# Loading the operands of a two-part sequence kernel through the crossbar transpose, with wide VectorE operations and a reordered prologue

## Chip, cores, metric

One core of one Trainium2 chip. The metric is device time of one execution in microseconds (us), lower is better; a figure for a kernel is the median of its executions. The kernel before takes 432.6 us (431.3 to 433.7). The profile is of one execution. The engines are PE (TensorE matmul), DVE (VectorE), ACT (ScalarE), POOL (GpSimd) and SP (SyncE, which here does nothing but issue loads).

## The reference, cut to what matters

Two independent parts are computed in one launch, all in bf16, S = 2048 positions, D = 1024 channels.

```python
# part A: 4-tap convolution of k, product with v, long convolution by FFT, product with q
for t in range(4): k_shift += k_pad[:, t:t+S, :] * shift_k[:, 3-t]
kv  = k_shift * v
y   = irfft(rfft(kv, 2S) * rfft(ssm_k, 2S))[:S] + kv * ssm_D
a   = q * y
# part B: diagonal complex state-space layer with 1024 states
Lam_bar = exp(dt * Lam);  B_bar = ((Lam_bar - 1) / Lam)[:, None] * Bmat
h_t = Lam_bar * h_{t-1} + B_bar x_t          # scan over the 2048 positions
y_t = 2 Re(C h_t) + x_t * Dskip
out = concat(a, y)
```

## The kernel before

Part B works on 16 chunks of 128 positions. For each chunk PE multiplies x by B ("u matmuls", tile `pu`), DVE rotates u by a table, runs a scan and rotates back (giving `h`), and PE multiplies `h` by C ("y matmuls", tile `py`). Part A runs in three stages: 16 rows of taps on DVE (`acc`) with first transforms (A1), a middle stage with 32 groups (A2: matmuls, a product on DVE with two halves swapped by a DMA, matmuls), and a last stage (A3). Both parts are laid into "ticks" (steps of the program's own schedule), and each engine executes its instructions in program order. B, C and x must reach PE with the contracted axis on partitions, so they have to be transposed.

```python
def b_load_x(i):                                   # x, before: plain load, PE transpose, ACT copy
    xn = xpool.tile([P, D], BF16, name="xn", bufs=3)
    dma(xn[:], x[i * T:(i + 1) * T, :])            # dma = a load issued by SP
    # ...
def b_xT(i, eng="s"):
    # ...
    for dd in range(ND):
        nc.tensor.transpose(pt[:, dd, :], xn[:, dd * P:(dd + 1) * P], ident[:])
    nc.scalar.copy(xT[:], pt[:])                   # or nc.vector.tensor_copy
# B (16 blocks) and C (16 blocks) likewise: bt_prep, ct_load / ct_prep

# rotation of one chunk: 12 operations of 1024 elements, two scans, small ones
nc.vector.tensor_mul(st["ta"][:], u[:, 0, :, :], ci[:])
nc.vector.tensor_mul(st["tb"][:], st["u"][:, 1, :, :], si[:])
nc.vector.tensor_add(st["ta"][:], st["ta"][:], st["tb"][:])
# ... three more, then
nc.vector.tensor_tensor_scan(fl(st["ta"]), fl(rtab), fl(st["ta"]), 0.0, ALU.mult, ALU.add)
# ... the scan of tb, the carry, and six more of 1024 for the rotation back

# taps of one row: 4 multiplies and 3 adds of 1024, then the product with v

# prologue: x(0) and B one block at a time, u of chunk 0 behind them; the parameters
# and tables between; then the tap rows and the filter rows (hk)
b_xT(0, "v")
for j in range(NJ):
    bt_prep(j, 0, "v"); bt_prep(j, 1, "s")
    if j >= 1: b_u(0, j - 1, 0); b_u(0, j - 1, 1)
    if j == 1: params_rest()
# ...
gen_tables_b()
```

## Time and profile before

| | before |
|---|---|
| time | 432.6 us (431.3 to 433.7) |
| PE busy | 380.7 us (88%) |
| DVE busy | 350.7 us (81%) |
| ACT busy | 303.6 us (70%) |
| first rotation of part B begins | 37.3 us |
| A2 (second stage of part A) begins | 190.4 us |

No engine is full all along, so the total shares say little; the span has to be cut into stages. First, of the page of the kernel before: the busy lines, and the rows that cut the span into 40 slices of 10.8 us, each digit the busy share in tenths.

```profile
PE 380.7 (88%) x3713; PEld 259.7 (60%) x3713; DVE 350.7 (81%) x642; ACT 303.6 (70%) x531; POOL 130.2 (30%) x224
...
PE   2589799797987997999899999999899999997784
...
DVE  2989999999999999936897979797959637976830
...
GB/s 247 285 255 309 336 289 254 265 240 249 276 235 205 167 163 159 120 334 238 229 241 263 217 247 245 265 234 295 195 217 181 165 69 135 298 176 396 403 316 73
```

DVE reads 8 or 9 from the second slice to the seventeenth (11 to 183 us), PE mostly 9 afterwards. The same in four windows chosen by milestones (prologue; the stage of taps and rotations; the end of A1; A2 to the last matmul). After the window and its length come busy us of PE, PEld, DVE, ACT and POOL with counts, then the granted clock, the DMA share and GB/s.

```profile
0.00:40.00 40.00, 24.48 (x320) 22.32 (x321) 29.26 (x97) 25.86 (x43) 5.32 (x13) 0.91 0.83 267
40.00:180.00 140.00, 123.09 (x1437) 96.35 (x1435) 138.56 (x238) 117.16 (x197) 66.58 (x102) 0.98 0.71 235
180.00:190.40 10.40, 10.40 (x133) 8.04 (x131) 3.98 (x10) 3.26 (x5) 0.00 (x0) 1.00 0.69 225
190.40:425.40 235.00, 222.41 (x1833) 132.98 (x1831) 178.92 (x299) 156.72 (x286) 57.80 (x108) 0.99 0.72 239
```

From 40 to 180 us DVE works 138.6 of 140 us: that stage is DVE-bound. From 190 us on PE works 222 of 235. What the change wants to remove is in these groups (count, busy us, mean ns of one): the transposes of B, C and x on PE, the copy of x on ACT, and narrow DVE operations.

```profile
L409 DVE TENSOR_TENSOR m<-krow,wbc 128x1024 bf16<-128x1024 bf16 x48 | 32.4, 675 | 0.0
...
L263 ACT COPY xT<-pt 128x1024 bf16<-128x1024 bf16 x15 | 15.9, 1060 | 1.7 <-PE pt L259 1.7
...
L601 PE MATMUL pt<-ident,bn 128*128 128x128 bf16 x128 | 12.4, 258 | 6.4 <-ACT BT L605 3.6 <-DMA bn<-in_B_B_im_dram 1.9 <-DVE BT L603 0.6
...
L618 PE MATMUL pt<-ident,bn 128*128 128x128 bf16 x128 | 10.6, 219 | 2.3 <-DMA bn<-in_B_C_im_dram 1.1 <-DMA bn<-in_B_C_re_dram 1.1
L259 PE MATMUL pt<-ident,xn 128*128 128x128 bf16 x128 | 10.3, 225 | 1.1 <-DMA xn<-in_B_x_dram 1.1
```

The loads are issued by SP's queue. Its timeline (start, length of the issue) shows that a plain 256 KB load holds that queue for 0.3 to 0.6 us:

```profile
3.14 0.36 SPq L85 DMA_DIRECT2D xn<-in_B_x_dram  x1
3.54 0.43 SPq L85 DMA_DIRECT2D bn<-in_B_B_re_dram  x1
4.02 0.59 SPq L85 DMA_DIRECT2D bn<-in_B_B_im_dram  x1
```

### The profile page before, as it was taken

To read this page: it belongs to the slowest core of one execution; us is meant where nothing else is said; L and a number is where in the kernel's file an instruction comes from. 1 tells how busy PE (TensorE), PEld (TensorE's weight loads), DVE (VectorE), ACT (ScalarE), POOL (GpSimd) and SP (SyncE) were. 2 spreads that over 40 slices of the span, in tenths; PEclk is the share of its full clock that TensorE was granted. 3 is DMA by queue.
4 is the path that set the end of the run, shared out by engine and by line. 5 is a ranking of instruction groups with operands and counts; after the bars stand their busy time and mean duration, and the time that the engine had idled before them with its cause. 6 is when DMAs were issued, how large, how long until landed. Compare 5 with 4: busy or idle time off the path is not lost.

```text
span 431.1 us, 9757 instructions
## 1 busy us (share of the span) xinstructions
PE 380.7 (88%) x3713; PEld 259.7 (60%) x3713; DVE 350.7 (81%) x642; ACT 303.6 (70%) x531; POOL 130.2 (30%) x224
## 2 busy tenths in 40 slices
PE   2589799797987997999899999999899999997784
PEld 2578687575765875775556566566465666763331
DVE  2989999999999999936897979797959637976830
ACT  1977999787886887646678877878568783344451
POOL 4000344464654455311222232322122211012121
PEclk9979999999999899999999999999899999999989
DMA  7879987778776544397778687879666523959981
GB/s 247 285 255 309 336 289 254 265 240 249 276 235 205 167 163 159 120 334 238 229 241 263 217 247 245 265 234 295 195 217 181 165 69 135 298 176 396 403 316 73
DMA packets 41353, 102.23 MB, mean 237 GB/s; under 512 B 6621, under 2 KB 8925, under 8 KB 41306
## 3 DMA queue, kind: packets, MB, share of 16 engines
q1 hardware_dynamic: 27322, 58.60, 42.7%
q0 software_dynamic: 13984, 43.01, 28.8%
q8 instruction: 29, 0.48, 0.5%
q14 instruction: 18, 0.15, 0.1%
HBM read 59.64 MB, written 33.55 MB: 216 GB/s over the span
## 4 chain that ended last, share of the span: by engine, by line
PE 42%; DVE 28%; issue 12%; DMA 10%; ACT 5%; POOL 2%; SPq 0%; POOLq 0%; DVEq 0%; ACTq 0%
PE pu L274 13%; PE py L345 13%; DVE m L409 5%; PE psa L508 5%; DVE acc L410 4%; DMA hb<-ha 3%; PE psa L533 3%; PE psa L532 3%; DVE ta L305 2%; DVE tb L308 2%; DVE acc L414 2%; DMA out_dram<-ot 2%; POOL out_dram L88 2%; DMA bn<-in_B_C_re_dram 1%; PE pt L601 1%
## 5 line engine op out<-in xcount | busy, mean ns | idle before, releaser
L274 PE MATMUL pu<-xT,BT 128*128 128x128 bf16 x2048 | 156.1, 222 | 0.5 <-ACT xT L263 0.3
L274 PEld LDWEIGHTS <-BT 128*128 128x128 bf16 x2048 | 136.2, 100 | 33.5 <-issue 2.4
L345 PE MATMUL py<-CT,h 128*128 128x512 bf16 x512 | 140.2, 382 | 2.3 <-ACT yo L355 2.3
L345 PEld LDWEIGHTS <-h 128*128 128x128 bf16 x512 | 46.7, 98 | 45.5 <-issue 4.9
L88 POOL DMA_DIRECT2D hb<-ha x64 | 33.4, 526 | 88.9 <-ACT ha L509 85.0
L534 ACT CAST vsb<-psa 128x512 bf16<-128x512 f32 x64 | 37.0, 602 | 25.7 <-PE psa L533 24.8
L88 POOL DMA_DIRECT2D Ys_h<-ysbh x64 | 45.6, 716 | 30.8 <-ACT ysbh L475 29.4
L277 ACT CAST u<-pu 128x512 bf16<-128x512 f32 x64 | 39.4, 615 | 13.2 <-PE pu L274 13.1
L428 ACT CAST ysb<-psa 128x512 bf16<-128x512 f32 x64 | 38.5, 644 | 13.7 <-PE psa L427 13.3
L519 DVE TENSOR_TENSOR ha<-x,ha 128x1024 bf16<-128x1024 bf16 x32 | 21.9, 684 | 27.8 <-DMA hb<-ha 18.7
L475 ACT CAST ysbh<-psa 128x512 bf16<-128x512 f32 x64 | 38.7, 641 | 5.5 <-issue 2.3
L509 ACT CAST ha<-psa 128x512 bf16<-128x512 f32 x64 | 36.8, 598 | 7.3 <-PE psa L508 6.3
L509 ACT CAST x<-psa 128x512 bf16<-128x512 f32 x64 | 36.9, 593 | 7.3 <-PE psa L508 5.2
L308 DVE TENSOR_TENSOR_SCAN tb<-rtab,tb 128x1024 bf16<-128x1024 f32 x16 | 36.6, 2285 | 0.0
L305 DVE TENSOR_TENSOR_SCAN ta<-rtab,ta 128x1024 bf16<-128x1024 f32 x16 | 36.5, 2280 | 0.0
L427 PE MATMUL psa<-acc,F1t 128*128 128x512 bf16 x64 | 24.6, 392 | 12.0 <-DVE acc L414 11.9
L564 ACT CAST ot<-psa 128x512 bf16<-128x512 f32 x32 | 17.9, 589 | 24.4 <-DMA out_dram<-ot 14.8
L409 DVE TENSOR_TENSOR m<-krow,wbc 128x1024 bf16<-128x1024 bf16 x48 | 32.4, 675 | 0.0
L410 DVE TENSOR_TENSOR acc<-acc,m 128x1024 bf16<-128x1024 bf16 x48 | 32.3, 673 | 0.0
L532 PE MATMUL psa<-ha,wts 128*128 128x512 bf16 x64 | 24.5, 384 | 4.2 <-DVE ha L519 4.0
L88 POOL DMA_DIRECT2D Ys_kv<-ysb x32 | 17.8, 557 | 33.9 <-ACT ysb L428 33.9
L350 PE MATMUL py<-Dd,xT 128*128 128x128 bf16 x128 | 28.0, 219 | 0.0
(139 smaller groups left out, 628.5 us busy)
## 6 DMA issues: line engine op xcount, KB each, us to landing
Ys_kv<-ysb POOLq DMA_DIRECT2D x32, 256.0 KB, 2.9
Ys_h<-ysbh POOLq DMA_DIRECT2D x64, 128.0 KB, 3.3
l2k<-Ys_kv SPq DMA_DIRECT2D x16, 512.0 KB, 6.0
l2h<-Ys_h SPq DMA_DIRECT2D x16, 512.0 KB, 4.2
hb<-ha POOLq DMA_DIRECT2D x64, 128.0 KB, 3.7
Vs<-vsb POOLq DMA_DIRECT2D x16, 512.0 KB, 5.9
vv<-Vs SPq DMA_DIRECT2D x32, 256.0 KB, 6.6
xn<-in_B_x_dram SPq DMA_DIRECT2D x16, 256.0 KB, 4.3
```

The costliest lines, as they stand in the source:

```text
L88: return nc.gpsimd.dma_start(out_, in_)
L274: nc.tensor.matmul(pu[:, c, jl, :], BT[:, j, c, dd, :], xT[:, dd, :], start=(dd == 0), stop=(dd == ND - 1))
L277: nc.scalar.copy(u[:, :, j - 1:j + 1, :], pu[:])
L305: ops.append(lambda: nc.vector.tensor_tensor_scan(fl(st["ta"]), fl(rtab), fl(st["ta"]), 0.0, ALU.mult, ALU.add))
L308: nc.vector.tensor_tensor_scan(fl(st["tb"]), fl(rtab), fl(st["tb"]), 0.0, ALU.mult, ALU.add)
L345: nc.tensor.matmul(py[:], h[:, c, j, :], CT[:, j, c, dh * 512:(dh + 1) * 512], start=(j == 0 and c == 0), stop=(j == NJ - 1 and c == 1))
L409: ops.append(lambda jj=jj: nc.vector.tensor_mul(st["m"][:], krows[n2 - jj][:], wbc[:, jj, :]))
L410: ops.append(lambda: nc.vector.tensor_add(st["acc"][:], st["acc"][:], st["m"][:]))
L428: nc.scalar.copy(ysb[:, dh * 512:(dh + 1) * 512], pt[:])
L475: nc.scalar.copy(ysbh[:, :, n2l, :], pt[:].rearrange("p (c d) -> p c d", c=2))
L509: nc.scalar.copy(d_[:, dh * 512:(dh + 1) * 512], pt[:])
L532: nc.tensor.matmul(pt[:], wts[:, gi, 1, :], ha[:, dh * 512:(dh + 1) * 512], start=True, stop=False)
```

## The change

The intent: take 384 of 512 transposes off PE and their copies off ACT by loading x, B and C through the DMA's crossbar transpose (a load that transposes its data on the way in); do the rotations and taps in fewer, wider DVE operations; and fill the prologue with three chunks of u and three tap rows instead of one chunk. The step lengths of A1, A2 and A3 in ticks are set anew. The diff, cut to its core:

```diff
+    def b_load_x(i):
+        xT = xpool.tile([P, ND, T], BF16, name="xT", bufs=XT_BUFS)
+        nc.sync.dma_start_transpose(xT[:], x[i * T:(i + 1) * T, :])
+    def bt_load(j, c):
+        nc.sync.dma_start_transpose(BT[:, j, c, :, :], Bv[c][:, j, :])
+    def ct_load(c, hf):                                   # four loads of 1 MB
+        nc.sync.dma_start_transpose(CT[:, :, c, hf * 512:(hf + 1) * 512], Cv[c][hf * 512:(hf + 1) * 512, :])
-    def b_xT(i, eng="s"): ...   def bt_prep(j, c, eng): ...   def ct_prep(c, dd, eng): ...
@@ rotation: one multiply of 4096 by a table window, one add of 2048, instead of six of 1024
+            s_ = src[:].rearrange("p b j t -> p (b j t)").unsqueeze(1).to_broadcast([P, 2, 2 * W])
+            nc.vector.tensor_mul(m, s_, win(Z))
+            nc.vector.tensor_add(g, m[:, :, 0, :], m[:, :, 1, :])
@@ taps: four rows of k in a ring, one multiply of 4096, an add of 2048, an add of 1024
+            nc.vector.tensor_mul(st["m"][:, 0:h0, :], kring[:, s0:s0 + h0, :], wbc[:, 0:h0, :])
@@ A2 product: x16 by both halves in one multiply of 2048
+        nc.vector.tensor_mul(hab[:], x16[:].unsqueeze(1).to_broadcast([P, 2, D]), hab[:])
@@ steps (ticks): taps 2 -> 3, filter 2 -> 2.5, A2 2 -> 1.5, A3 1 -> 2; chunks of u in the prologue 1 -> 3
@@ prologue: loads of x(0..2) and all of B first; three tap rows on POOL's queue; then
+    params_pre(); gen_tables_a(); run(kvo(0)); params_rest()
+    pro_u(0); pro_mm(0); params_tabs(); run(kvo(1)); gen_tables_b()
+    pro_u(1); pro_mm(1); run(kvo(2)); pro_u(2); pro_mm(2); pro_u(3)
+    a1h_load(0)                                           # filter rows, behind 19 crossbar loads
+    for n2 in (3, 4): a1_load_k(n2, dma); a1_load_v(n2, dma)
+    for hf in range(2):
+        for c in range(2): ct_load(c, hf)
```

## The prediction

> **What bounds it now.** No single engine. The page gives PE 88%, DVE 81%, ACT 70% of 431 us. The table of stretches splits this: from 40 to 180 us DVE is at 19.2-20.0 of every 20 us while PE has 16-19.6 (the stage of conv taps plus state-space rotations: DVE-bound); from 180 to 360 us PE is at 17.6-20.0 and DVE at 7.6-18 (PE-bound, DMA share about 0.8 at 250 GB/s); before 40 us (PE 24.5 of 40, chain of waits through loads of B, PE transposes, ACT copies of BT and wbc) and after 380 us (PE 38 of 51, DMA 0.7-0.8) nothing is full. PE's true occupancy, from back-to-back cadences in the chain (16 pu matmuls 0.89 us, 4 py matmuls 0.86 us, 8 transposes 0.62 us), is an estimate of 369 us, so PE is the floor.
>
> **What the change does.**
> - PE: 384 of 512 transposes (x, B, C) go, about 27 us by cadence; 8 wbc broadcast matmuls come, +2. Estimate 369 -> 343 us.
> - ACT: xT, CT, BT, wbc copies go (15.9+18.0+8.1+4.1 us), 8 small wbc copies come: 304 -> about 263.
> - DVE: a 1024-wide bf16 multiply starts every 0.60 us in the timeline, of which, by the 128-wide ones (0.16-0.25 us), about 0.07 is fixed: 4096 wide = estimate 2.2 us, 2048 = 1.13. Rotation of one chunk: 12x0.60 + two scans (4.6) + 8 tiny ops, about 12.7 -> 2.2+1.13+4.5+2.2+1.13+0.25 = 11.5. Taps of one row 4.8 -> 4.5. Product 1.2 -> 1.13. All DVE: about 348 -> 322.
> - DMA: same bytes (12 MB now through the transpose path). The Trainium skill, "DMA: Bandwidth & Descriptors", section "Latency and other measured facts", gives 261 GB/s for DMA transposes with a non-contiguous middle dimension, about 350-400 contiguous; no trace of this case shows it yet. With the 250-310 GB/s that plain loads reach here, I estimate at most +10 us of DMA time, spread out.
> - Order: three u chunks and three kv rows in the prologue; products step 1.5 ticks instead of 2, the final output stage step 2 instead of 1, so it overlaps the state-space part to the end.
>
> **On the critical path.** Prologue: about 39 us as before until the first rotation, but with two more u chunks and about two more kv rows done (10-14 us gained). DVE-bound stage: 13x4.5 + 5.5x11.5 = 121 us instead of 140 or so; second stage starts near 175 us instead of 190. After it PE has an estimated 183-190 us and DMA 57 MB at 285-300 GB/s (190-200 us): both nearly full, about 205 us with losses. Total about 386 us.
>
> **Predicted** 386 us, 80% range 370 to 410. Faster by over 2%: 0.92; within 2%: 0.05; slower: 0.03.
>
> **What would show it.** Group list: no transposes but those of hk; 4096-wide multiplies at 2.2-2.3 us; scans unchanged. Stretches: PE over 15 of 20 us from 10 us on, DVE full to about 165 us, PE full afterwards, PE over 17 of 20 in the last 50 us. DMA issues: transposed 256 KB loads landing in 4-7 us.
>
> **What would make it wrong.** Crossbar transposes far slower (landing over 10 us, starving PE in the prologue); a C load (1 MB) arriving late and blocking the in-order PE; DMA saturating in the second half because A2 is now denser; wide operands with a repeated dimension losing the two-per-cycle rate (4.3 us each: then slower than before).

## The result, and the profile after

The changed kernel takes **445.9 us** (444.8 to 447.9), against 432.6 us of the kernel before on the same chip: ratio 1.031, 95% interval 1.025 to 1.037. It is slower by 3%; the prediction had given that 3 chances in 100. Ratios here and below are the mean time of one kernel's fast runs over the mean of the kernel before's fast runs of the same rounds, so they are not quite the ratio of the medians quoted.

The groups did about what was predicted. From the page after (`q1` is the queue of SP's loads: packets, MB, and the share of 16 engines' span that they took): less busy time on every computing engine, the wide operations at their estimated lengths, no transposes but those of the filter.

```profile
PE 358.7 (81%) x3293; PEld 240.7 (54%) x3337; DVE 329.5 (74%) x336; ACT 267.8 (60%) x500; POOL 136.3 (31%) x236
...
PE   0290964988969896999699998899897989997793
...
DVE  0816799991999999999468593956859497799621
...
GB/s 148 221 189 233 220 270 259 307 199 251 192 167 284 216 98 193 140 148 184 300 209 210 293 229 246 261 216 345 236 286 235 207 158 95 203 367 316 311 386 104
DMA packets 83850, 101.12 MB, mean 228 GB/s; under 512 B 56148, under 2 KB 58340, under 8 KB 83809
...
q1 hardware_dynamic: 69232, 56.19, 49.2%
...
L341 PE MATMUL pu<-xT,BT 128*128 128x128 bf16 x2048 | 144.3, 226 | 30.6 <-DMA xT<-in_B_x_dram 14.2
...
L359 DVE TENSOR_TENSOR mt<-u,Z 128x4096 bf16<-128x4096 bf16 x16 | 36.6, 2288 | 0.3
```

PE's busy time fell by 22.0 us on the page (nearer 17: this trace lacks 44 of its 3337 matmul records, and e4, which has the same matmuls and all records, shows 363.5), DVE's by 21.2, ACT's by 35.8, and still the span grew by 11.9 us (431.1 to 443.0): what grew is waiting. The row of PE shows where: the first five slices read 0, 2, 9, 0, 9 (and 6 and 4 next) instead of 2, 5, 8, 9, 7, and the u matmuls alone waited 30.6 us, nearly all for loads of x and B. The windows, with the same milestones:

```profile
0.00:40.00 40.00, 13.86 (x137) 10.86 (x137) 14.24 (x64) 15.85 (x31) 11.67 (x25) 0.95 1.02 185
40.00:180.00 140.00, 111.23 (x1285) 89.27 (x1301) 126.33 (x117) 85.21 (x158) 51.75 (x80) 0.93 0.82 223
180.00:215.70 35.70, 30.66 (x351) 23.23 (x353) 34.36 (x29) 23.20 (x42) 15.20 (x23) 0.97 0.58 184
215.70:436.00 220.30, 202.80 (x1523) 117.34 (x1548) 153.91 (x127) 142.71 (x270) 56.59 (x106) 0.97 0.82 250
```

In the first 40 us PE works 13.9 us instead of 24.5, DVE 14.2 instead of 29.3. The DMA engines are busy all that time (the records give a share of 1.02, over 1 because they overlap) and yet move 185 GB/s instead of 267. A2 to the last matmul is shorter, 220.3 us instead of 235.0, but begins 25.3 us later. SP's queue after shows how the prologue's loads stood in line:

```profile
2.20 1.34 SPq L133 DMA_TRANSPOSE xT<-in_B_x_dram  x1
...
10.99 4.76 SPq L139 DMA_TRANSPOSE BT<-in_B_B_im_dram  x1
15.79 4.81 SPq L133 DMA_TRANSPOSE xT<-in_B_x_dram  x1
...
36.98 1.31 SPq L139 DMA_TRANSPOSE BT<-in_B_B_im_dram  x1
38.33 1.05 SPq L85 DMA_DIRECT2D hk<-in_A_ssm_k_dram  x2
...
40.48 7.28 SPq L142 DMA_TRANSPOSE CT<-in_B_C_re_dram  x1
...
60.17 6.17 SPq L142 DMA_TRANSPOSE CT<-in_B_C_im_dram  x1
...
67.50 5.71 SPq L133 DMA_TRANSPOSE xT<-in_B_x_dram  x3
```

A crossbar load of 256 KB holds the queue for about 1.3 us at best, four times a plain one, 4.8 us at a time when POOL's loads of the tap rows are in flight (that they are the cause was not tested), and a 1 MB load of C for 5.7 to 7.3 us. A plain load isn't always short either: e13, below, has two of 1 MB that hold the queue for 4.8 and 3.1 us. So the filter rows (`hk`) are not asked for before 38 us and the next chunks of x not before 67 us. PE, which executes in order, stands before each of them. PE's longest waits in the trace after:

```profile
PE pu L341 <- DMA xT<-in_B_x_dram: 14.2, 2, 10.3
PE pu L341 <- DMA BT<-in_B_B_re_dram: 12.8, 2, 8.0
PE pt L483 <- DMA hk<-in_A_ssm_k_dram: 10.8, 1, 10.8
```

A second queue of waits adds to this. The parameters of part B need one small transpose on PE. It runs at 7.3 us before; after, it stands behind u matmuls that wait for B, and runs at 12.1 us. ACT's next parameter step stands behind a copy of u, which stands behind the rest of that block of B. ACT's timeline after (the bracket is the idle time before, and what ended it):

```profile
12.54 0.21 ACT L212 ACTIVATE dt<-p 128x8 bf16<-128x8 f32 x1 [10.51 <-DVE p L206]
24.00 0.59 ACT L344 CAST u<-pu 128x512 bf16<-128x512 f32 x1 [11.25 <-PE pu L341]
24.48 0.21 ACT L219 ACTIVATE r<-a__170 128x8 f32<-128x8 f32 x1
```

The tables come late, the taps that stand behind them on DVE begin at 42.9 us, and the first rotation begins at 59.9 us instead of 37.3. Its first operation, before and after:

```profile
37.31 0.68 DVE L292 TENSOR_TENSOR ta<-u,ci 128x1024 bf16<-128x1024 bf16 x1
...
59.90 2.28 DVE L359 TENSOR_TENSOR mt<-u,Z 128x4096 bf16<-128x4096 bf16 x1
```

### The profile page after: what moved, and what is told of

It is laid out like the page before. It is cut to its first block, busy times and chain, and to the rows that moved or that the text cites. A ratio compares the mean times of both kernels' runs of the same rounds, so it can differ in the third digit from the quotient of the medians.

```text
span 443.0 us, 8543 instructions
## 1 busy us (share of the span) xinstructions
PE 358.7 (81%) x3293; PEld 240.7 (54%) x3337; DVE 329.5 (74%) x336; ACT 267.8 (60%) x500; POOL 136.3 (31%) x236
## 2 busy tenths in 40 slices
DMA packets 83850, 101.12 MB, mean 228 GB/s; under 512 B 56148, under 2 KB 58340, under 8 KB 83809
## 3 DMA queue, kind: packets, MB, share of 16 engines
q1 hardware_dynamic: 69232, 56.19, 49.2%
## 4 chain that ended last, share of the span: by engine, by line
PE 29%; DVE 24%; DMA 14%; issue 12%; SPq 10%; ACT 7%; POOL 3%; POOLq 0%; DVEq 0%; ACTq 0%
PE pu L341 11%; PE py L402 9%; DMA hab<-hab 6%; SPq L139 6%; DVE mt L359 4%; DVE g L377 4%; DVE mt L431 4%; DMA Ys_h<-ysbh 3%; DVE mt L438 2%; PE psa L540 2%; DVE hab L548 2%; SPq L133 2%; POOL out_dram L88 2%; PE psa L559 2%; DVE acc L445 1%
## 5 line engine op out<-in xcount | busy, mean ns | idle before, releaser
L341 PE MATMUL pu<-xT,BT 128*128 128x128 bf16 x2048 | 144.3, 226 | 30.6 <-DMA xT<-in_B_x_dram 14.2
L377 DVE TENSOR_TENSOR_SCAN g<-rtab,g 128x1024 bf16<-128x1024 f32 x32 | 72.4, 2282 | 0.3
L548 DVE TENSOR_TENSOR hab<-x,hab 128x2048 bf16<-128x2048 bf16 x32 | 38.8, 1219 | 35.9 <-DMA hab<-hab 27.8
L88 POOL DMA_DIRECT2D hab<-hab x64 | 33.4, 526 | 58.2 <-ACT hab L541 41.6
L541 ACT CAST hab<-psa 128x512 bf16<-128x512 f32 x64 | 36.3, 607 | 9.8 <-DMA wts<-a_c_W 4.3
L359 DVE TENSOR_TENSOR mt<-u,Z 128x4096 bf16<-128x4096 bf16 x16 | 36.6, 2288 | 0.3
L359 DVE TENSOR_TENSOR mt<-g,Z 128x4096 bf16<-128x4096 bf16 x16 | 36.5, 2282 | 0.1
L591 ACT CAST ot<-psa 128x512 bf16<-128x512 f32 x32 | 18.5, 590 | 26.8 <-DMA out_dram<-ot 12.7
L559 PE MATMUL psa<-hab,wts 128*128 128x512 bf16 x62 | 24.3, 391 | 9.1 <-DVE hab L548 8.7
L389 DVE TENSOR_TENSOR h<-mt 128x2048 bf16<-128x2048 bf16 x16 | 19.6, 1222 | 15.1 <-PE py L402 14.8
L431 DVE TENSOR_TENSOR mt<-kring,wbc 128x4096 bf16<-128x4096 bf16 (+3 forms) x16 | 30.2, 1887 | 0.3
L506 PE MATMUL psa<-hT,F1t 128*128 128x256 bf16 x128 | 22.4, 272 | 9.8 <-ACT ysbh L507 5.0
```

Source lines behind the costliest of these rows:

```text
L88: return nc.gpsimd.dma_start(out_, in_)
L341: nc.tensor.matmul(pu[:, c, jl, :], BT[:, j, c, dd, :], xT[:, dd, :], start=(dd == 0), stop=(dd == ND - 1))
L359: nc.vector.tensor_mul(m, s_, win(Z))
L377: nc.vector.tensor_tensor_scan(g[:, a * W:(a + 1) * W], rt1, g[:, a * W:(a + 1) * W], 0.0, ALU.mult, ALU.add)
L431: nc.vector.tensor_mul(st["m"][:, 0:h0, :], kring[:, s0:s0 + h0, :], wbc[:, 0:h0, :])
L541: nc.scalar.copy(d_[:, dh * 512:(dh + 1) * 512], pt[:])
```

## The experiments

The theories at the outset. The **crossbar** theory (T1 in the quoted texts): crossbar loads are slower and hold SP's queue, and everything behind them is late. Rivals: the **order** of the new prologue (three chunks of u before the first rotation; later sharpened to "theory P": the parameter chain and filter rows stand behind u work and B loads in in-order queues); the **wide** DVE operations with their dependences; the new **step lengths**. All runs of one call share a chip and the runs of the kernel before; the calls (e1 to e4, e5 to e8, e9 to e12, e13 to e15, e16) were on three chips, so a step from one call to another is taken from the ratios. Every run below was correct except e13 and e14, which are wrong. e12's two milestones are not compared with others. One core has no second core to compare with, so the state is judged by the spread of runs alone. Medians are of all runs, ratios of the fast ones; counted as slow were 2 of 4 in e6, 1 of 4 in e7 and in e8, 4 of 6 in e9, 1 of 6 in e11, 3 of 6 in e12 and 2 of 6 in e15.

| run | what it is | median us | ratio (95%) | first rotation at | A2 starts at |
|---|---|---|---|---|---|
| before | | 432.6 | 1 | 37.3 | 190.4 |
| after | | 445.9 | 1.031 (1.025-1.037) | 59.9 | 215.7 |
| e1 | before + crossbar loads | 440.2 | 1.020 (1.014-1.026) | 35.5 | 196.2 |
| e2 | after, transposes on PE | 445.9 | 1.033 (1.028-1.038) | 61.5 | 224.9 |
| e3 | before + wide DVE work | 428.7 | 0.994 (0.987-1.001) | 36.1 | 188.7 |
| e4 | after, C later | 435.8 | 1.008 (1.002-1.014) | 62.1 | 208.2 |
| e5 | e4, parameters and filter rows first | 427.3 | 0.988 (0.981-0.995) | 50.5 | 201.6 |
| e6 | e3, x through the crossbar | 435.9 | 1.002 (0.990-1.014) | 39.1 | 189.4 |
| e7 | e3, new step lengths (taps 2.5) | 429.5 | 0.992 (0.983-1.001) | 36.1 | 202.1 |
| e8 | after, one chunk in the prologue | 439.0 | 1.013 (1.004-1.022) | 61.1 | 218.4 |
| e9 | e5, one chunk in the prologue | 428.0 | 0.977 (0.969-0.986) | 50.0 | 199.0 |
| e10 | e2, parameters first, one chunk | 447.6 | 1.034 (1.029-1.039) | 53.5 | 224.6 |
| e11 | e3, 30 unread plain loads | 456.9 | 1.053 (1.047-1.059) | 39.9 | 217.0 |
| e12 | e3, 30 unread crossbar loads | 466.1 | 1.070 (1.062-1.078) | 40.9 (slow) | 227.2 (slow) |
| e13 | after, all crossbar loads plain (wrong result) | 416.4 | 0.964 (0.959-0.968) | 46.7 | 193.2 |
| e14 | e5, all crossbar loads plain (wrong result) | 415.8 | 0.961 (0.958-0.965) | 47.7 | 195.1 |
| e15 | e4, parameters first alone | 432.4 | 0.995 (0.988-1.002) | 50.2 | 207.1 |
| e16 | e7, C through the crossbar | 422.2 | 0.974 (0.969-0.979) | 36.8 | 198.8 |

### First four: one part of the change at a time

**e1, the crossbar alone in the old kernel.**

```diff
-        dma(xn[:], x[i * T:(i + 1) * T, :])            # + PE transposes, + ACT copy; B and C alike
+        nc.sync.dma_start_transpose(xT[:], x[i * T:(i + 1) * T, :])
```

> The kernel before with only the loads of x, B and C changed to crossbar transposes (their PE transposes and copies gone; narrow DVE work, old order, old schedule). Theory T1 (a 256 KB crossbar load holds the sync queue 1.3 us instead of 0.33 and moves at about 190 GB/s, so the prologue starves): first rotation no earlier than the 37 us of before, probably 40 to 50, PE idle in the first 60 us; but 30 us of PE work is gone later, so total 425 to 445. Rival T2 (the wide DVE instructions are what cost) expects this one clearly faster than before: about 405 to 415. Rival T3 (the new schedule and prologue order) likewise: 405 to 415.

It took 440.2 us, 2% slower than before, although PE is relieved of 384 transposes and ACT of their copies. The first rotation keeps its place (35.5 us), so here the loss comes later: in the first 100 us PE waits for B (16.1 us), C (10.7 us) and the filter rows (8.4 us), and A2 starts 5.8 us later than before. The crossbar costs time in the old order too.

**e2, the changed kernel with the transposes on PE again.** There was no room for the staging tiles of before, so x, B and C share three.

```diff
-        nc.sync.dma_start_transpose(BT[:, j, c, :, :], Bv[c][:, j, :])
+        bn = bnpool.tile([P, D], BF16, name="bn", bufs=3); dma(bn[:], Bv[c][:, j, :])
+        # ... 8 PE transposes into PSUM, a copy by DVE or ACT into BT; x and C alike
```

> The changed kernel with x, B and C loaded plainly and transposed on PE again (two transpose banks and three psa banks as before; one x buffer and one k row less, which the SBUF needs). T1: prologue recovers, first 4096-wide rotation near 40 us instead of 60, total 415 to 430. T2: no better than the changed kernel plus the added 27 us of PE work: 445 or more. T3: also 440 or more, because order and steps stay.

445.9 us: no gain, a miss for the crossbar theory as it was stated. But the run isn't clean. Here the first u is complete only when all of B has come through three staging tiles, with two more chunks interleaved, and the first rotation begins at 61.5 us with a wait for u. It put one cause in place of another.

**e3, the wide DVE operations alone in the old kernel.**

```diff
-            nc.vector.tensor_mul(st["ta"][:], u[:, 0, :, :], ci[:])     # and 11 more of 1024
+            rot_mul(state.pop(("u", i)), Z1)                            # 4096, then an add of 2048; twice
-    six multiplies/adds of 1024 and more per tap row, two products per A2 group
+    the wide forms of the change (u buffers 5 -> 4, staging shared, to fit)
```

> The kernel before with only the wide DVE work (two-op rotations, 4096-wide taps, 2048-wide products). T1 and T3: within 2% of before, if anything a little faster, 422 to 434, because DVE saves some 20 us of busy time but each dependent op waits about 0.1 us for the one before. T2: slower than before, 440 or more.

428.7 us, the same within the interval. So the wide operations do no harm, and little good, though DVE's busy time fell by 15.5 us (350.7 to 335.2). A likely part of the reason is in the timeline of e3 (start, length): an operation that reads the one before it starts later than one that does not.

```profile
50.03 2.28 DVE L402 TENSOR_TENSOR mt<-kring,wbc 128x4096 bf16<-128x4096 bf16 x1
52.34 1.23 DVE L409 TENSOR_TENSOR mt<-mt 128x2048 bf16<-128x2048 bf16 x1
53.60 0.69 DVE L416 TENSOR_TENSOR acc<-mt 128x1024 bf16<-128x1024 bf16 x1
```

The wide multiply to its dependent add is 2.31 us, the add to the next 1.26 us. In the trace of e13, with independent work behind it, the same multiply is followed after 2.21 us. One tap row alone in its chain takes 4.92 us (36.8 to 41.7 us in e13, 50.0 to 54.9 in the changed kernel), not the predicted 4.5. The Trainium skill, "VectorE: DVE Perf Modes", section "The DRAIN you can't avoid", reports eight copies that took no longer with a semaphore after each; here an operation that reads the one before it starts about 0.1 us later than one that does not. That the wait on the result is what costs it was not tested by itself.

**e4, the changed kernel with C later.** The order of SP's queue changes, and C's four loads of 1 MB become sixteen of 256 KB.

```diff
-    for hf in range(2):
-        for c in range(2): ct_load(c, hf)                 # 4 x 1 MB in the prologue
+    # 16 crossbar loads of 256 KB, two per tick, in the first eight ticks
```

> The changed kernel with the four 1 MB crossbar loads of C cut into sixteen of 256 KB and moved into the first eight ticks, behind the fourth chunk of x. T1: the 10.4 us wait of PE for that x chunk (62 to 73 us in the trace of after) goes or shrinks, total 432 to 441, first rotation unchanged at 58 to 61 us. T2 and T3: no change, 443 to 449.

435.8 us: 10 us of the 13 us loss are gone, with no work removed. Place and size of C's loads changed together, so the 10 us belong to both. The loads of C had stood before x's next chunks and everything else. The first rotation is no earlier (62.1 us).

### Order, one chunk, step lengths

**e5, parameters and filter rows first.** On top of e4, `hk` is asked for before the crossbar loads, and one tiny matmul that reads the finished table stands before the first u matmul, so the parameter chain passes PE and ACT before any u work.

```diff
+    for t_ in range(2): dma(hk0[:, t_, :], A_ssm_k[t_ * P:(t_ + 1) * P, :])   # before b_load_x(0)
+        if i == 0 and j == 0 and c == 0:
+            nc.tensor.matmul(pu[0:8, 0, 0, 0:8], Z1[:, 1, 0, 0:8], Z1[:, 1, 0, 0:8], start=True, stop=True)
```

> The run with C later, plus: the first h rows are loaded before the crossbar loads, and one tiny matmul that reads the finished cosine table is put before the first u matmul (its result is overwritten), so that PE and ACT run the parameter chain before they wait for crossbar data. Theory P (in the changed kernel the parameter chain, and with it the first DVE work, stands in the in-order PE and ACT queues behind u work that waits for slow crossbar loads): ACT's table chain ends near 32 us instead of 42, first rotation near 48 to 52 us instead of 60 (it is behind three tap rows), total 422 to 431. Rival Q (the first half is limited by DMA and PE work anyhow): first rotation earlier, but total unchanged from the 435.8 of the run with C later, within 3 us.

427.3 us: another 8.6 us by the ratios, and now slightly faster than before. Order (with C's loads cut smaller), for the same bytes and the same arithmetic plus one tiny matmul, is worth 18.6 us.

**e6, the crossbar for x alone, on e3.**

```diff
-        dma(xn[:], x[i * T:(i + 1) * T, :])      # on e3
+        nc.sync.dma_start_transpose(xT[:], x[i * T:(i + 1) * T, :])
```

> Before plus the wide DVE work (the 428.7 us run) plus x alone by crossbar; B and C stay on PE. If crossbar loads are harmful only in the loaded first 80 us: 418 to 425, since 10 us of PE and 16 us of ACT work go, much of it in the PE-bound half. If they cost everywhere[...]: 428 to 436.

435.9 us with a wide spread (429.4 to 438.9); e3's interval and this one overlap. No gain is seen from taking 128 transposes off PE and 16 copies off ACT and DVE. The edit also leaves three staging tiles of four, now for B and C alone, and gives x one buffer more. No single wait explains it; unclear.

**e7, the new step lengths alone, on e3.** The taps step 2.5 ticks here and not the 3 of the change, whose first three rows lie in the prologue.

```diff
-    a1_step 2.0   a1h_step 2    a2_step 2    a3_step 1
+    a1_step 2.5   a1h_step 2.5  a2_step 1.5  a3_step 2
```

> Before plus the wide DVE work with the new spacing of stages (taps and h every 2.5 ticks, products 1.5, output 2), old prologue, no crossbar. If the spacing costs (theory S): 436 or more, near the changed kernel. If the spacing is neutral and the new prologue is what costs: 425 to 432. My prediction had taken it for a gain: 415 to 422.

429.5 us, the same as e3. A2 starts 13.4 us later (202.1 against 188.7) and from there to the last matmul's end takes 14.5 us less (217.7 against 232.2). These steps move work, they do not save any.

**e8, one chunk of u in the prologue of the changed kernel.**

```diff
-    U_PRO = cfg.get("u_pro", 3)
+    U_PRO = cfg.get("u_pro", 1)
```

> The changed kernel with one chunk of u in the prologue instead of three (x chunks 1 and 2 are then loaded after). If three chunks in the prologue are what delays PE and ACT (theory P'): parameter chain no longer behind x chunk 1, first rotation 50 to 55 us, total 432 to 440. If not: 444 to 452, as the u work only moves later.

439.0 us, about 8 us better by the ratios, as the theory had it; but not by its mechanism: the first rotation is no earlier (61.1 us), as B and the parameters stand as before, and A2 starts later (218.4 us). The gain lies after that: from A2 to the last matmul's end it is 212.2 us, against 220.5 in the changed kernel. Why was not tested.

**e9, the same in e5.**

```diff
-    U_PRO = cfg.get("u_pro", 3)      # in e5
+    U_PRO = cfg.get("u_pro", 1)
```

> e5 (C later, h-filter rows first, parameters ahead of u) with one u chunk in the prologue instead of three. Theory P (the loss is what stands ahead of the parameter chain and the first state-space work in in-order queues): e5 already removed most of it; the first rotation comes another 5 us or so earlier than e5's 50.5, and the time is 420-428 us. Rival (three chunks up front are useful work that has to be done anyway, and after e5 only the transfer rate of the crossbar binds the first 60 us): no gain, 427-433 us.

The median is 428.0 us, the runs spread from 419.9 to 431.0, and four of six were slow, so the ratio rests on two. The median shows no gain over e5, and the first rotation is where it was (50.0 us). Inconclusive.

**e15, e5's two parts split: parameters first, filter rows still behind.**

```diff
+        if i == 0 and j == 0 and c == 0:         # in e4: the tiny matmul alone
+            nc.tensor.matmul(pu[0:8, 0, 0, 0:8], Z1[:, 1, 0, 0:8], Z1[:, 1, 0, 0:8], start=True, stop=True)
```

> e4 (435.8 us) with the parameters ahead of u alone, the filter rows still behind the crossbar loads. If the parameter chain behind u is the larger part: 427-431 us and a first tap sum near 36 us as in e5. If the filter rows are: 433-436 us.

432.4 us: between. By ratios, 1.008 to 0.995 to 0.988 of 432 us: the parameters are worth some 6 us, the filter rows some 3. The intervals of neighbours overlap, so the split is rough.

### What does the crossbar itself cost?

**e10, e2 with the order mended.**

```diff
+    # e2 with the tiny matmul before u, and U_PRO = 1
```

> The changed kernel with x, B, C loaded plainly and transposed on PE again, parameters ahead of u, one u chunk in the prologue (three shared buffers for the plain loads). Theory (with the order mended, crossbar loads and PE transposes are worth about the same, because what they save on PE they cost on the load queue and in DMA time): 423-432 us, within 1.5% of e5's 427. Rival A (the crossbar is a net loss in any order): below 420 us. Rival B (the crossbar is a net gain once the order is right): above 432 us. First rotation below 45 us, against 61.5 in e2.

447.6 us, with the first rotation at 53.5: by the numbers Rival B. The trace doesn't bear it out: from 20 to 40 us the DMA share is 0.40, and between 15 and 100 us SP's queue waits 17.5 us for PE to free a staging tile of B. The run measures three staging tiles, not the crossbar. A fair test needed the transposes gone without anything in their place.

**e11 and e12, unread loads on top of e3.** The same 30 loads of 256 KB to a scratch tile, plain or through the crossbar. To make room, both have three staging tiles where e3 has four.

```diff
+        xs = bnpool.tile([P, D], BF16, name="xs", bufs=1)
+        dma(xs[:], x[i * T:(i + 1) * T, :])                       # e11
+        nc.sync.dma_start_transpose(xs3d, x[i * T:(i + 1) * T, :])  # e12
```

> The kernel with only the wide VectorE work (e3, 428.7 us), plus 30 plain 256 KB loads of x rows from the same queue that nothing reads. If plain DMA traffic has room: 429-435 us; each extra load holds the queue about 0.4 us.

> As e11, but the same 30 unread loads go through the crossbar transpose. PE, ACT and VectorE work is the same as in e11, so the difference is the price of the crossbar loads alone. If that price is real away from the prologue too: each holds the queue 1.3 us or more and the time is 6-15 us above e11. Rival (the crossbar costs only where work waits on it in the prologue): within 3 us of e11.

e11 took 456.9 us, far more than either figure on record. The design was at fault: with one scratch tile each load has to wait for the one before, and SP's queue stood 38.0 us in 16 such waits (49.1 us in 20 in e12, in a slow run), with every other load behind. So e11 can't be read as the price of plain traffic; it shows again how dear a halt of this queue is. Their difference, 0.017 in ratio or about 7 us for 30 loads, is the price of the crossbar there, about 0.25 us a load, and a rough one, because half of e12's runs count as slow.

**e13 and e14, plain loads in place of crossbar loads, nothing else.** The result is wrong (B, C and x are used untransposed). Every instruction on PE, DVE and ACT is the same, and so are the tiles and the bytes. The busy times agree too: DVE 329.3 us in e13 against 329.5, ACT 268.3 against 267.8, PE 359.0 against 358.7.

```diff
-        nc.sync.dma_start_transpose(BT[:, j, c, :, :], Bv[c][:, j, :])
+        dma(BT[:, j, c, :, :].rearrange("p d t -> p (d t)"), Bv[c][:, j, :])    # x and C alike
```

> The changed kernel with plain loads of the same bytes to the same tiles for x, B and C (wrong result on purpose; no other instruction changes). If the loss is the crossbar's slow transfers and long queue holds, to which the order of the prologue only adds: the first rotation moves from 59.9 us to about 40-45 us, the start of the second stage from 215.7 to 190-200 us, and the time is 415-428 us. Rival (the order is the whole loss, the crossbar no more than a plain load): 440-446 us.

> The same replacement in e5 (C later, filter rows first, parameters ahead of u: 427.3 us). Theory: with the order mended the crossbar costs less, 5-10 us: 415-422 us here. Rival (nothing left to gain from the transfers): 425-430 us. My prediction's 386 us, if its account of all but the loads was right, should be near here: below 400 us. If it is not, then the mis-sizing of the second half is separate from the crossbar.

e13 took 416.4 us: the crossbar loads cost the changed kernel 0.068 of 432 us, or 29 us. e14 took 415.8 us: in e5's order they cost 0.027, or 11 us. And e13 and e14 are equal: with plain loads this change of order doesn't matter. So it isn't crossbar or order. The crossbar makes a load slow and the queue slow, and the order decides how much of that falls on work that waits. Some lines of SP's queue in e13, to be held against those after:

```profile
2.20 0.36 SPq L85 DMA_DIRECT2D xT<-in_B_x_dram  x1
...
20.30 0.33 SPq L85 DMA_DIRECT2D BT<-in_B_B_im_dram  x1
21.02 1.72 SPq L85 DMA_DIRECT2D hk<-in_A_ssm_k_dram  x2
...
37.77 2.21 SPq L85 DMA_DIRECT2D xT<-in_B_x_dram  x3
```

And e13's windows, with its own milestones:

```profile
0.00:40.00 40.00, 24.77 (x296) 21.02 (x298) 25.01 (x80) 24.87 (x49) 13.23 (x28) 0.91 0.97 325
40.00:180.00 140.00, 122.39 (x1345) 94.37 (x1360) 136.34 (x119) 95.47 (x173) 62.44 (x97) 0.96 0.62 206
180.00:193.20 13.20, 9.41 (x137) 7.94 (x137) 13.01 (x10) 4.32 (x8) 3.10 (x5) 0.95 0.76 253
193.20:409.60 216.40, 202.44 (x1523) 116.57 (x1548) 154.25 (x130) 143.68 (x271) 56.77 (x107) 0.97 0.79 256
```

In the first 40 us the same DMA engines, as busy as before (0.97 to 1.02), move 325 GB/s instead of 185. The filter rows are asked for at 21 us instead of 38, the next x at 38 instead of 67. From e13's page, against 56148 packets under 512 B and a share of 49.2% for `q1` in the changed kernel:

```profile
DMA packets 42313, 101.12 MB, mean 243 GB/s; under 512 B 6419, under 2 KB 12707, under 8 KB 42272
...
q1 hardware_dynamic: 27696, 56.18, 42.1%
```

For the same bytes the crossbar makes 49,729 more packets under 512 B, and SP's loads take 218 us of all 16 engines (49.2% of 443.0) instead of 175 (42.1% of 415.6). In the packet records of the trace after, the crossbar's are 256 B each with a median of 18 ns, a plain packet of 2048 B takes 84 ns: 1.7 times the time for a byte.

But e14 was also to be below 400 us if all else in the prediction was right, and e13 and e14 stand at 416. The other half of the miss has nothing to do with the crossbar.

### A version that beats both

**e16, the crossbar only where there is slack.** The old prologue, which transposes B and x on PE while PE is idle anyway, the wide operations, the new steps, and C alone through the crossbar after the prologue.

```diff
-        dma(cn_[:], Cv[c][dd * P:(dd + 1) * P, :])     # on e7; + 8 transposes, + ACT copy
+        nc.sync.dma_start_transpose(CT[:, :, c, dd * P:(dd + 1) * P], Cv[c][dd * P:(dd + 1) * P, :])
```

> e7 (old prologue, wide VectorE work, new step lengths: 429.5 us) with C alone loaded through the crossbar, as 16 loads of 256 KB in the first ticks after the prologue. If the price of the crossbar is paid where work waits on it, C with its slack of some 20 us should pay little and PE saves 128 transposes (about 9 us of busy time, not all of it on the critical path): 420-428 us. Rival (crossbar loads slow every other load of that stage as well): 429-436 us.

422.2 us (419.6 to 424.6), 2.6% faster than before, and correct. The sixteen loads hold SP's queue for 1.3 to 4.1 us each between 40 and 69 us, and the y matmuls that need C begin 3.5 us later than in e7 (63.5 against 60.0 us), but A2 starts 3.3 us earlier than there.

## Why the prediction was wrong

The miss can be put on stages, by milestones of the profiled runs: the first rotation; A2's first matmul; A3's or part B's last matmul; the end. The prediction's row uses its own figures (39, second stage at 175, then 205), with the rest to 386 as the tail. The cuts before the tail are those of the windows above; they lie within 0.7 us of the last matmul's end (425.8, 436.2 and 408.9 us). All in us.

| stage | predicted | before | after | e13 (no crossbar) |
|---|---|---|---|---|
| start to first rotation | 39 | 37.3 | 59.9 | 46.7 |
| first rotation to A2 | 136 | 153.1 | 155.8 | 146.5 |
| A2 to the last matmul | 205 | 235.0 | 220.3 | 216.4 |
| tail | 6 | 5.7 | 7.0 | 6.0 |
| span | 386 | 431.1 | 443.0 | 415.6 |

Of the 57 us between the prediction and the changed kernel's span, 27.4 are the step from e13 to after, and 29.6 the step from the prediction to e13 (7.7 before the first rotation, 10.5 from there to A2, 11.4 after).

- **Wrong: "DMA ... at most +10 us of DMA time, spread out".** This is the step that turned the sign. The text cited the Trainium skill, "DMA: Bandwidth & Descriptors", section "Latency and other measured facts" (261 GB/s for a transposing load with a non-contiguous middle dimension, 350-400 contiguous). Here 23 crossbar loads of 9.2 MB together took SP's queue from 2.2 to 66.3 us, or 143 GB/s with other loads between, and the whole DMA moved 185 GB/s in the first 40 us against 325 with plain loads. SP's loads cost 43 us more DMA time than in e13 (218 against 175), where 10 had been allowed; by the sum of their packet times the 12.6 MB went at an estimated 162 GB/s (77.7 us of all 16 engines), not 261. The same text's guess for a landing, 4 to 7 us, was right (median 5.2 us for x, 4.4 to 4.6 for B). Landing time was the wrong thing to look at: in e13 the plain loads of B landed later, after 8.5 to 9.4 us, and the kernel was faster. The price is in how long each load holds the queue (1.31 us and up, against 0.33 to 0.43) and in throughput, and it isn't spread out but falls in the first 75 us, where everything waits on loads. e13 puts it at 29 us.
- **Wrong: "about 39 us as before until the first rotation, but with two more u chunks and about two more kv rows done".** Measured 59.9 us. Some 13 us are the crossbar (46.7 in e13). The other 8 are, as the trace reads, the work put in front: in e13 DVE works without a break from 31.8 us on three tap rows of 4.9 us each that stand before the first rotation in its order. No run took them away. What was counted as a gain on top was to be paid in the same place.
- **Half wrong: "DVE-bound stage: 13x4.5 + 5.5x11.5 = 121 us", second stage 15 us later.** In e13 the last tap sum ends 124 us after the first rotation began, so the 121 held without the crossbar (132 with it; DVE is busy 120.7 us of that stretch in both, and the rest is waiting). But A2 then starts 22.5 us after that sum, not 15; before, it was 18.5. Why this drain grew wasn't tested.
- **Mis-sized: "an estimated 183-190 us" of PE in the second half, "about 205 us with losses".** PE is busy there 202.8 us in the changed kernel and 202.4 in e13, with 14 to 18 us idle (25 of 1548 matmul records are missing in both; e5, which has all, shows 203.4). The estimate, it seems, took PE's shortest cadences for a whole stage in which dependences and waits for the swapped halves (`hab`, 27.8 us of DVE waits in the changed kernel, 20.9 in e13) are part of the flow; no run tested that. The gain there, 14.7 us, is real, but e7 shows that the new steps take a like amount from before A2: they carry work over the boundary.
- **Right:** no transposes but the filter's; 4096-wide multiplies at 2.29 us (2.2-2.3 predicted), scans unchanged; ACT 267.8 us (263 predicted), DVE 329.5 (322). PE's fall was smaller, about 17 us (26 predicted). "A C load (1 MB) arriving late and blocking the in-order PE" and "Crossbar transposes far slower (landing over 10 us, starving PE in the prologue)" were named as what would make it wrong, and were given far too small a chance. The second happened, without the landing time that was named as its sign. The first didn't happen as written: PE never waits for C in the trace after. The C loads stood in SP's queue before x, and PE waited 10.3 us for that x.

What stays open: why the drain before A2 is longer, why one chunk in the prologue shortens the time after A2 (e8), what the changed PSUM banks do (transposes two to one, `psa` three to four; no run took them alone), why x alone through the crossbar brings nothing (e6), and how the 29 us divide between the transfer rate and the hold of SP's queue. The 43 us of DMA time are the size of the first; both were removed together in e13, and no run took one away without the other.

## What to carry to other kernels

A load path that saves an engine work isn't free because the byte count is the same: look at how many packets it makes, how long each load holds its issuing queue and which in-order work stands behind it, and test it by putting a plain load in its place, with a wrong result if need be, before building around it. Use the slow path where the data has slack (C after the prologue, e16), not where a whole kernel waits for its first operands. And a busy-time saving counts only in the stage whose limit it is; add the stages up one by one, and count work moved ahead of a milestone as a delay of that milestone.

## What the Trainium skill lacked or had wrong

- No page gives, for trn2 and loads of this size, the time a crossbar load holds its issuing queue. Here: about 1.3 us for 256 KB at best, up to 4.8 us with other loads in flight, 5.7 to 7.3 us for 1 MB; a plain 256 KB load mostly 0.33 to 0.43 us. It belongs to "DMA: Bandwidth & Descriptors", section "DMA Transpose (X-bar)".
- "DMA: Bandwidth & Descriptors", section "Issuing engines are not separate DMA queues", calls the time to initiate a DMA "usually small relative to the DMA itself". For crossbar loads it was not: 1.31 us of hold against 4.4 to 5.2 us from issue to landing, with everything behind in the queue delayed.
- "Advanced Engine Details and Errata", section "X-Bar Transpose (TRN2)", says "TRN2 transpose DMAs are as fast as regular DMAs". Not here: 185 GB/s in the first 40 us against 325 with plain loads of the same bytes, and 29 us of kernel time.
- "VectorE: DVE Perf Modes", section "The DRAIN you can't avoid", says of eight copies that a semaphore after each "costs nothing extra", and gives no figure for an operation that reads the result of the one before. Here a 4096-wide multiply is followed after 2.31 us by an operation that reads it and after 2.21 us by one that does not.
